# Where the unit matrix of an attention and feed-forward kernel is built: VectorE instead of GpSimd, with a new order and new buffer numbers

## The chip, the cores and the metric

The kernel runs on one core of a Trainium2 chip. A core has five engines that run beside each other, each through its own list of instructions in order: TensorE (PE in the profile, PEld for its loading of weights), VectorE (DVE), ScalarE (ACT), GpSimd (POOL) and SyncE (SP). They wait for each other through semaphores. POOL and SP, and at the end ACT, also issue DMAs. The metric is the time of one execution in microseconds (us); less is better. Several executions are given, and one more execution was recorded by the profiler.

## The reference

Attention with a decay by a forget gate, over 8 batches of 8 heads with 576 rows of 64, and behind it a gated feed-forward layer of width 1536 on the 4608 rows of 512 that come out:

```python
scores = scale * np.matmul(q, k.transpose(0, 1, 3, 2))
cum = np.cumsum(np.log(np.clip(f, 0.0001, 1.0)), axis=-1)
scores = np.where(causal, -1e9, scores + cum[:, :, :, None] - cum[:, :, None, :])
attn = np.exp(scores - np.max(scores, axis=-1, keepdims=True))
attn = attn / (np.sum(attn, axis=-1, keepdims=True) + 1e-09)
x = np.matmul(attn, v)                       # (B, H, S, D), then rows of H * D = 512
xn = x / np.sqrt(np.mean(x * x, axis=-1, keepdims=True) + 1e-06) * rms_g
g = xn @ w_gate
out = (g * (1.0 / (1.0 + np.exp(-g))) * (xn @ w_val)) @ w_out
```

## The kernel before

**A list of units.** The function builds 1956 units. A unit is a step on one engine with the units it depends on, an emitter that writes its instructions, and the buffers that it takes and gives back. Pieces of work in the code are named by what makes them: `load_qk` and `load_v` issue loads (q and k on POOL, L333 and L345 in the profile, v on SP or POOL, L356), `turn` transposes q and k by DMA from SP (L436), `turn_pe` transposes the first two batches' q and k on TensorE with the unit matrix (L451 and L457), `score_block` multiplies q and k (L526), takes the exponential on ScalarE (L545) and masks the diagonal block on POOL (L553), `scale_v` multiplies v with the decay (L486), `values` multiplies the weights with v (L574) and divides on VectorE (L593, L597), `norm` scales the rows (L619 to L636), `gate` makes the two products with w_gate and w_val (L831), and then `th` on ScalarE (L843) and two steps on VectorE, `ga` (L845) and `hT` (L838); `seven` does the same for the later groups with seven products in place of eight (L766 to L817), and `project` makes the last product (L909) with its sums on VectorE (L919) and copies on ScalarE (L916).

**The order is written out by hand.** `ORDER` gives each unit, in the order in which they are built, its rank in one list, as a number of two letters. `Plan.run` walks through the units by rank, and each engine gets its own instructions in that order. No engine can do a later unit before an earlier one of its own.

**The buffers are written out too.** A `Hold` is one use of one buffer out of a ring: `ff` are banks of PSUM for TensorE's results (4, and 8 once the scores are done and their ring `sc` is given back), `qk` 12 tiles that the loads of q and k fill, `th`, `ga`, `PT`, `xn`, `x`, `ores` and others are tiles in SBUF. `SLOTS` has one digit (or letter) for each of the 1298 Holds in the order in which the units were built: which buffer of its ring it gets. Two of the rings, `hw` and `sw`, are lanes for DMAs in the plan alone and stand for no memory. Whoever writes into a buffer waits until all who used it in its former use have ended; that is how a digit becomes a wait. Walked through by rank, the digits of before give out the free buffer of the ring that has been free longest: this holds for all rings, with 4 exceptions among the 333 banks and one on each of the two lane rings.

**A gate's banks.** A `gate` takes two Holds of `ff`, `hg` for the product with w_gate and `hv` for the one with w_val. `hg` is given back by `ga`, which comes after `th`; `hv` by `hT`, which comes after `ga`.

**The start.** f is loaded first on SP. Its decay runs through VectorE (L283), ScalarE's Ln (L285), VectorE's running sum (L291 and after) and ScalarE's Exp (L300); TensorE turns it with the fp32 unit matrix `ident_f` (L309). The transposes of q and k need the bf16 one, `ident`. Before, `make_identity` on POOL fills `ident_f` with a memset (masks.py:197) and an affine_select (masks.py:199), behind four DMA issues and ahead of the fifth; `mhalf`, a constant of -0.5, is set behind it (L271), and VectorE casts `ident_f` to `ident` (L274).

Of the kernel before, what the change touches and what calls it, by code (L numbers as in the profile page):

```python
# [32 lines left out]
WEIGH_ACT = "gv"  # L33
LETTERS = string.digits + string.ascii_letters
ORDER = (
    "0302000105060407080e090r0w0j0m0p0q0x0f0g0D1u120a0b0h0i0c0d0n0o0k0l0u0v0J0K0F0G0N0O0z0A14151v1w1G1H26"
    "272A2B2m2n35363m3n0V0W0s0t1Q1R1l1m1a1b0R0S2T2U2h2i3b3c3h3i2Y2Z3r3s3w3x3Y3Z4q4r45465q5r3N3O4x4y5R5S4L"
    "4M505164654T4U4F4G6h6i6l6m6d6e7B7C6O6P6B6C8n8o7j7k6V6W7H7I70718k8l7P7Q8V8W7p7q9U9V9C9D7N7Oa7a8b9baak"
    "alaDaEaBaC9M9N9w9xapaqbCbDadaebjbkc0c1bGbHdrdscgchdkdlcxcycEcFfsftcNcObqbrdVdWexeydadbdedfdEdFdzdAgb"
    "gceYeZeUeVgqgrg1g2fEfFgmgnf1f2e2e3g8g9hrhsgNgOjcjdiuivhDhEhShThQhRjajbiziAiniohkhljUjViXiYhxhyh0h1kv"  # L40
    "kwkgkhl4l5kLkMkQkRlElFlHlIlxlymmmn0y0C0B0E0I0H0M0Z0P0T0L0Q0Y1019131g1s1h1j1p1q1t1A111c1d1f1k1z1D1K1P"
    "1Z1V211C1N0U0X2G2s2j252a2u2f20231I1O472p2v2L2y2P302V3T3t393k3v3V4p4f4k41424a4b3M4V5f5a4B4C4O4P615x5E"
    "5I5H5N6a60695i5j55566q6k5c5d5u5v6F6g6p6v6A5C5D5K5L7F6M747b6Y7c7i7r7y67685W5X8e7D7K7R7Z8784896K6L7d7e"
    "948d8r8j7m7n75769o9b8C8K939c9h7U7V7u7v8N9j9u9p9v81829q9r9F9J9Oa29A9B9H9IaIanaFaOavaLaPaWa0a1ahaib2b4"
    "bbbgbfbnbSbsbWbxbyaRaSbvbZb5b6asataxcecmcscwaYaZcqcrbLcMcYd3cQdhdndwdKcAcBcIcJdidTdZedeietepeudOdPer"
    "eseMeCeHeXd5d6e0e1fXcff9fnfufrfAe8e9elemf8fDfPfLfQf5f6fkfldUg0gdg7fdfeezeAi0gugBgYgDgPgZgUfUfVggghhN"
    "hphIi4hzhWihieiigFgGh3h4gThLgzgAgKgLiTitiFiMixhXhYibicjAiSiWjgj8jrjujzjHj2j3iOiPl8jPjSk1k4kpkekUiGiH"
    "jNjOkGkzkPkFjXjYjCjDknlvkYlblClglnksktkCkDlOlulJlBm4kVkWl9lalVlXm3m9lhlilLlMnmmfmkmsmpmymFmImtmumgmh"
    "nzmTn4ndn1nenknhnv1618171e1n1x1o1y1L1X1S1W292e2g2o2O2R3234383g3e3l4t4z4E4Y4R534Z575Q6b6o6x6J796Z777G"
    "7T7X858a8g8h8m8q8t8v8z9n9t9G9K9L9Qa3a9aJaQb8blbmbtbpbwbzbEc8cjcPcUcXd1dgdjdxdCegejeEeLePeSf0f4fBfJge"  # L50
    "giglgHgsgygJgVhohthAhGiwiIiNiViUj0jEjMjRjWk7kdkfkokqkAkHkKlklzlAlPlQm8lZm5memimomEmwmBmHmPn3ncnJnMo6"
    "oaomot1i1r1B1F1J1E1M1T1Y22282d2l2t2x2E2I2M2S2XcKeGgji6i73B3E3I3X4Q4W3R4l4u5Y5T626G6Q6T6f6H6X98cnk6kb"
    "kc8u8f8x929e9f8G8L8M8w8D8H8O8Y8Z8Q9697a6acd7eeefaAaVaXbPbUbVb3c2c3bFbKbOccckclc6cacbfjfohakkkldLdIdR"
    "eaeNeOeTfyfzfcfafhfxfHfIfCfNfOhmiamCn9nahdh8hghUipiqhFhJhKi1j1j6jljojpjejvjwkal2ldlRlSk3kxkBkXlsltl6"
    "m6m7l0lUmzmNmRmSmMmYmZntnEpXpZq0mXnbnip4pppqo7oLoMnXoeoiosp0p1oNoToUq1qpqEqIqJ1U2k242b2r2c2w2q2z2D2C"
    "2F2H2K2N333D3q3A3J3P3a4m3f664K5t5y2J3j2Q313p3y3Q3H3S3W2W3u373d3C3o3L3z3F43583K4X494S524A44484v4j4n4J"
    "3G4h3U4c4s4o4I4w4D5e404e4d4g4i6y4H6U5p7f6R6N6u5z6c5M5U6j5g6s5B5G6D7l7L7x7E7W788y7A7M8F636w6n6r6E5b5l"
    "5m5s5w727w7a7g7J7S837Y888b8s8E8A8P918R9g959i9m7h7s7o7t7z868i8c8p8BbRcic9cdcp9P9Z9W9Ya4a5ajagamarb0bh"
    "b7bdboabazaoayaHbubJbAbIbTczcRcHcLd09TaNaaawbebBbNbMbQbXcocGcvcDddbYcuc5c7cCauaGaKaMaUf3gxfffmgEcZdm"
    "d4d8dvevfbeDf7fidteqdDdSewdNenekeBeFd9dJdudydQfSgofYgagtfvfWfGfRg3d2dBdcdodHeIfpeQeWfwgRh2h6h9hedGe5"  # L60
    "dMe4echOifidigimgIh7gMgShciJj9iQj7jjhiilhvi2iyhbhChqhwhMhHhZhPhVi5hfhuhjhnhBj4jTjkjxk8iZjmj5jqjtjyjL"
    "jGjIjQi3jsi9iCjBgCgWgQgXh5llmLmVnwk2njnQn2nAmAmGnPlTnunynDnLnGnKnTo2o4oco5ojnpnIodoknSnZo9oHoloooKow"
    "nOnYonozohoQoBoGmOnlmUn8nqk9l7kmkrljmrnNmxmQo0kEl1kIkOlcngnxnonBnHkulNkNlflWlGmalYmbmvlomjlwlDmqnFnV"
    "oCorpIpLpCpFpUq2q8q7qeqmqcqypPpYqlqoqdqaqkqwquqAqPqFqbqjqCqKqzqTqHqMnCnRoqoynWofovpgoAoFpjoPnUo3p2pd"
    "obouoEpkp5prpopBo1ogoWpHr1r5pfpuo8opoOoRoxoJp7p6pipAptpKoDoVpwpzpyoYpcpMpspJpQqioIpGpOqspTqhq4q9pVqg"
    "qNqqq3qfqrqvqBqnqtqYqQqVrdr9rcrfrjrsrorkrnryrtrzrCrFr7rJrirHsisls1s5qGqOr0r4qUr2rargrmrprlrvqDqRr6rq"
    "r3qWqZrNrerurVrBqXr8rKrMsasprArDrrrwrRrUrGrErLs9sesksgsorWs6suswsvsjsnsGsxsAsLsOrXsHsKsVsMsQsBsDrbrx"
    "sCrTrPs0rSsfstshsqsssEsJsSthsTsYsNsXt6t3t7tktdtgtstpsyt9tttytatxtltotwtAtmtqtKtEtGtztQtUtJtYtFtPtTu9"
    "u4tWu3ufukusuiuCtNuuuguPtSunujuvsRsWsZt2t1t8tftetLtRtnu2tbtitHtZtutrtvuhtOu5uluttctBuyuNuduqucue4N5A"
    "59805h5J5n5O545k5o5P8T8U5F5Z5V6t6z6I9R9S6S739k9l909acVcW8I9d8Saf8J8X9z9Xdpdq999y9s9EaTb1ijikbcbieJeK"  # L70
    "c4ctcScTdYeoe6fTdXe7ebehg4g5fgfqeRfMfKfZiDiEg6gkgvgwgfgpjhjihhisiLiRi8iriBiKjJjKjfjnjFjZk0k5lplqkiky"
    "mcmdkSkZm0m1kjlKl3lrkJkTlelmn6n7m2mlmDmJmKn0p8p9n5nnnrnsmWnfq5q6oXp3papeoSoZpbphplpmpvpxpnpDpEpNpRpS"
    "pWqxuaubqLqSsbscrhrZrQs2rIrOrYs4s7s8s3sdsmsrszsFuLuMsUt0t4t5sIsPu6u7tjtDtMuztCtItVtXu0u1u8uoumurupux"
    "uAuBuGuSuVuWuwuFuJuKuEuQuIuYuDuHuRuXv1v2uZv0uOuTuUv4v3v6v9vavhviv7vgvkvlvnvovjvrvuvvvwvxv5v8vdvevbvc"
    "vfvmvpvqvsvt")
SLOTS = (
    "751b7a63624352207908611307523743413263122050114766530534220172616310531a3810792b42666701745572212243"
    "5338606b7011595a02420533041643272850316b41377033792a11060370412562024453190b11565a707768322423423b52"
    "015566330970324741101a182264036302557113221173001561043120301100167312010541010321067011001454310732"
    "1011601200501741054321001017350016201454210702130011340016133105410107201036201610170147161105455103"  # L80
    "6012064017101456710360130101220107031014525101610234001071050230142011463106310204610751061560134137"
    "0101207107054016537011401320201071060352042231221111001352140030230101224125321243053200153343503020"
    "1235300110352232340353111431320223421335110022113311201203304200320110220163127152120231071011314170"
    "5261420107310025311042735031060220313133111010032113300020023002111001131111110030020011311003003311"
    "2200110113110110101113112100100130012010113111010331030102101021120010310210003011200121103101030132"
    "1013110201011012002110131002010301231013100231112113301030000100311130112000200131120163451704341012"
    "0110210010000012101301112113100051040720161115630227647015206514613001657356472010032116403740051617"
    "0760211043235670610104017671415011244056532102102430322217412120004531311261321023230243076222101235"
    "20120232612014360203173122105235354314317120731055051054421034363034027512103206507321410743523656")
# [66 lines left out]
def fox_ffn_kernel(ctx, tc, q, k, v, f, moe_w_gate, moe_w_val, moe_w_out, moe_rms_g, out):  # L156
    nc = tc.nc
    B, H, S, D = q.shape
    assert (B, H, S, D) == (8, 8, 576, 64)
# [114 lines left out]
    iden = dve(0.23, -19, lambda: nc.vector.tensor_copy(ident, ident_f), [iden_f])  # L274
# [10 lines left out]
    d2 = act(0.7, -19, lambda: nc.scalar.activation(fr, fr, ACT.Ln), [d1])  # L285

    def emit_cum():
        ones = bass.AP(tensor=one.tensor, offset=one.offset, ap=[one.ap[0], [0, S]])
        nc.vector.memset(one, 1.0)
# [3 lines left out]
        nc.vector.tensor_scalar_mul(mid, mid, 0.5)  # L293
# [6 lines left out]
    d4 = act(0.9, -19, lambda: nc.scalar.activation(dec[:, 0:S], cum, ACT.Exp, scale=-1.0, bias=mid[:, 0:1]),  # L300
             [d3])
# [761 lines left out]
```

## Time and profile before

| | us |
|---|---|
| median of 3 executions | 357.12 |
| lowest and highest | 354.87, 357.41 |
| the profiled execution, its own time | 354.97 |
| its span, first to last instruction | 353.1 |

The mean granted clock of TensorE in the profiled execution is 0.995 of full speed. In the profile "x4314" is a number of instructions, "PE ff L831" is TensorE writing the tile ff from line 831 of the kernel, and "<-" in a wait names what ended it. An idle time in brackets stands ahead of an instruction. A row by stage has the stretch, its length, and then the busy time of PE, PEld, DVE, ACT and POOL with the number of instructions, the granted clock, the DMA share (over 1 where the engines hold more than one packet each) and GB/s. The end of a matmul is modelled, so a busy PE need not be PE at its peak. Buffer numbers are left out in the profile; which bank a matmul writes is read from SLOTS.

### The profile page before, as it was taken

The page shows a single profiled execution, that of the slowest core. Times are in us where ns is not written, and L with a number is a line of the kernel's source. Part 1 is how long each engine was busy: PE and PEld are TensorE (multiplying, and loading weights), DVE is VectorE, ACT ScalarE, POOL GpSimd, SP SyncE. Part 2 cuts the span into 40 slices and gives each one's busy share as a digit, 9 for nine tenths or more (in the row PEclk, how much of TensorE's full clock was granted, in tenths as well). Part 3 has the DMA queues.
Part 4 walks back from the last instruction along what each step waited for, and adds up shares of the span by engine and source line. Part 5 has one row for each costly group of instructions (what it writes and reads, how often), then busy time and mean ns, then how long its engine had stood idle before and what let it go on. Part 6 is the DMA issues. An engine that isn't in the chain of part 4 may idle for free.

```text
span 353.1 us, 10559 instructions
## 1 busy us (share of the span) xinstructions
PE 334.1 (95%) x4314; PEld 259.9 (74%) x4314; DVE 275.9 (78%) x507; ACT 266.6 (75%) x440; POOL 205.8 (58%) x247
## 2 busy tenths in 40 slices
PE   1699999999999999999999999899999999999995
...
DMA  9999999899999999999999999963013200100225
GB/s 126 205 215 226 188 184 132 154 162 158 111 161 177 148 147 172 178 127 159 149 163 162 170 171 116 163 136 87 23 23 89 69 7 2 62 7 24 93 90 148
DMA packets 159464, 44.88 MB, mean 127 GB/s; under 512 B 145012, under 2 KB 158840, under 8 KB 159416
## 3 DMA queue, kind: packets, MB, share of 16 engines
...
q8 instruction: 33, 0.54, 0.7%
...
## 4 chain that ended last, share of the span: by engine, by line
PE 79%; POOL 6%; DVE 5%; DMA 4%; issue 2%; ACT 1%; SPq 1%; DVEq 0%; POOLq 0%
PE ff L831 29%; PE ff L909 16%; PE late L766 9%; PE ff L766 8%; PE ff L574 6%; PE sc L526 6%; PE late L909 5%; DMA qk<-in_k_dram 2%; DMA xT<-xn 1%; POOL qk L333 1%; ACT PT L545 1%; DMA v<-in_v_dram 1%; POOL PT L553 1%; DVE hT L838 1%; POOL Vs L486 1%
## 5 line engine op out<-in xcount | busy, mean ns | idle before, releaser
L545 ACT ACTIVATE PT<-sc 128x1024 bf16<-128x1024 f32 x96 | 94.9, 1021 | 15.8 <-PE sc L526 15.6
L831 PE MATMUL ff<-xT,wv 128*128 128x128 bf16 (+2 forms) x464 | 68.6, 291 | 0.6 <-DVE hT L838 0.4
L831 PE MATMUL ff<-xT,wg 128*128 128x128 bf16 (+2 forms) x464 | 68.0, 291 | 0.7 <-DVE ga L845 0.5
L817 POOL TENSOR_TENSOR hT<-PT,PT 128x512 bf16<-128x512 f32 x20 | 25.9, 1301 | 53.6 <-ACT PT L811 33.0
L845 DVE SCALAR_TENSOR_TENSOR ga<-th,ff 128x512 f32<-128x512 f32 x68 | 46.1, 682 | 12.3 <-ACT th L843 11.2
L838 DVE SCALAR_TENSOR_TENSOR hT<-ga,ff 128x512 bf16<-128x512 f32 x68 | 46.0, 684 | 11.2 <-PE ff L831 10.0
L553 POOL TENSOR_SCALAR_AFFINE_SELECT PT<-PT 128x1024 bf16<-128x1024 bf16 x32 | 37.3, 1166 | 27.1 <-ACT PT L545 26.9
L843 ACT ACTIVATE th<-ff 128x512 f32<-128x512 f32 x68 | 39.8, 595 | 13.5 <-PE ff L831 8.8
L831 PEld LDWEIGHTS <-wg 128*128 128x128 bf16 x464 | 36.4, 98 | 18.5 <-issue 0.8
L831 PEld LDWEIGHTS <-wv 128*128 128x128 bf16 x464 | 36.1, 98 | 18.3 <-issue 0.9
L909 PEld LDWEIGHTS <-hT 128*128 128x128 bf16 x432 | 41.4, 98 | 5.9
L486 POOL TENSOR_TENSOR Vs<-v,decT 128x512 bf16<-128x512 f32 (+1 forms) x30 | 33.1, 1105 | 18.8 <-DMA v<-in_v_dram 18.7
L574 PEld LDWEIGHTS <-PT 128*128 128x128 bf16 (+1 forms) x896 | 32.0, 102 | 9.5 <-issue 2.8
L574 PE MATMUL ff<-Vs,PT 128*128 128x65 bf16 (+1 forms) x896 | 36.8, 196 | 1.3 <-POOL Vs L486 0.9
L597 DVE TENSOR_TENSOR x<-ff,rden 128x256 f32<-128x256 f32 (+1 forms) x80 | 33.9, 424 | 2.7
L909 PEld LDWEIGHTS <-sm 128*128 128x128 bf16 x324 | 31.2, 98 | 6.1 <-issue 1.3
L526 PE MATMUL sc<-QT,KT 64*128 64x128 bf16 (+1 forms) x960 | 32.8, 212 | 0.7 <-ACT PT L545 0.6
L526 PEld LDWEIGHTS <-KT 64*128 64x128 bf16 x960 | 24.0, 96 | 10.9 <-issue 9.0
L333 POOL DMA_DIRECT2D qk<-in_q_dram x34 | 29.9, 882 | 0.8 <-POOLq L1047 0.8
L333 POOL DMA_DIRECT2D qk<-in_k_dram x34 | 29.9, 880 | 0.1
L909 PE MATMUL ff<-wo,hT 128*128 128x256 bf16 x240 | 29.3, 273 | 0.0
L919 DVE TENSOR_TENSOR ores<-ores,ff 128x512 f32<-128x512 f32 (+1 forms) x35 | 23.4, 669 | 7.6 <-PE ff L909 7.2
...
## 6 DMA issues: line engine op xcount, KB each, us to landing
...
wo<-in_moe_w_out_dram POOLq DMA_DIRECT2D x2, 768.0 KB, 10.5
```

What stands on the lines that cost most here:

```text
L333: nc.gpsimd.dma_start(out=T_qk[h.slot][0:n, :].rearrange("p (h d) -> p h d", d=D), in_=src[b, :, p0:p0 + n, :].rearrange("h p d -> p h d"))
L486: eng.tensor_tensor(T_Vs[hv.slot][0:n, j, :, 0:D], T_v32[h.slot][0:n, :, :], bcast(dj, D), ALU.mult)
L526: nc.tensor.matmul(t[:, par, c:c + n], lhsT=kt[r, p, kj * 128:(kj + 1) * 128], rhs=qt[r, p, qi * 128:qi * 128 + n], start=not x, stop=True ...
L545: nc.scalar.activation(T_of_p[hp.slot][:, 0:2 * half].rearrange("p (a c) -> p a c", a=2)[:, :, 0:cols], T_sc[h.slot][:, :, 0:cols], ACT.Ex ...
L553: nc.gpsimd.affine_select(out=d, in_=d, pattern=[[0, 8], [1, n]], compare_op=ALU.is_ge, fill=0.0, base=0, channel_multiplier=-1)
L574: nc.tensor.matmul(T_ff[hpo.slot][r0:r0 + n, p * 65:p * 65 + 65], lhsT=T_of_p[h.slot][:, c:c + n], rhs=vs[:, kj, 2 * p + par, :], start=(k ...
L766: nc.tensor.matmul(t[:, c * HTK:(c + 1) * HTK], lhsT=w[:, d, (2 * u + c) * 128:(2 * u + c + 1) * 128], rhs=r[:, d, :], start=(start and c ...
L831: nc.tensor.matmul(T_ff[h.slot][:, c:c + n], lhsT=w[:, dc, fc * 128:(fc + 1) * 128], rhs=xT[:, dc, t0:t0 + n], start=(dc == 0), stop=(dc = ...
L838: nc.vector.scalar_tensor_tensor(hT, in0=three[0], scalar=0.5, in1=three[1], op0=ALU.mult, op1=ALU.mult)
L843: th = act(0.6, key - 0.1, lambda: nc.scalar.activation(T_th[ht.slot], T_ff[hg.slot], ACT.Tanh, scale=0.5), [ug], take=[ht])
L845: a = dve(0.69, key - 0.1, lambda: nc.vector.scalar_tensor_tensor(T_ga[ha.slot], in0=T_th[ht.slot], scalar=1.0, in1=T_ff[hg.slot], op0=ALU ...
L909: nc.tensor.matmul(t[:, s * HD:(s + 1) * HD], lhsT=a()[:, fc, s * 128:(s + 1) * 128], rhs=w[:, fc, :], start=(not more and s == ss[0] and ...
```

## The change

The unit matrix is built on VectorE. A running count along the columns (a scan over ones) gives 1 to 32 in each row, a transpose of blocks of 32x32 gives the same count down the rows, and where the two are equal the bf16 matrix gets a 1; four such comparisons fill the four blocks on the diagonal of a zeroed tile. `ident_f` is cast from `ident`, where before it was the other way. `mhalf` is set on VectorE too, and the memset of `one` moves there from `emit_cum`, which now depends on this unit. POOL has no part of it any more.

```diff
-from concourse.masks import make_identity
...
-    one = sb.tile([BH, 1], F32, name="one")
+    one = sb.tile([128, 1], F32, name="one")
+    diag = sb.tile([128, 64], F32, name="diag")
...
     def emit_ident():
-        make_identity(nc, ident_f)
-        nc.gpsimd.memset(mhalf, -0.5)
-
-    iden_f = pool(0.7, -15.5, emit_ident)
-    iden = dve(0.23, -19, lambda: nc.vector.tensor_copy(ident, ident_f), [iden_f])
+        along, down = diag[:, 0:32], diag[:, 32:64]
+        nc.vector.memset(one, 1.0)
+        ones = bass.AP(tensor=one.tensor, offset=one.offset, ap=[one.ap[0], [0, 32]])
+        nc.vector.tensor_tensor_scan(along, ones, ones, 0.0, ALU.mult, ALU.add)
+        nc.vector.transpose(down, along)
+        nc.vector.memset(ident, 0.0)
+        for c in range(0, 128, 32):
+            nc.vector.tensor_tensor(ident[c:c + 32, c:c + 32], along[c:c + 32, :], down[c:c + 32, :], ALU.is_equal)
+        nc.vector.memset(mhalf, -0.5)
+
+    iden = dve(1.2, -25, emit_ident)
+    iden_f = dve(0.2, -19, lambda: nc.vector.tensor_copy(ident_f, ident), [iden])
...
     def emit_cum():
-        ones = bass.AP(tensor=one.tensor, offset=one.offset, ap=[one.ap[0], [0, S]])
-        nc.vector.memset(one, 1.0)
+        ones = bass.AP(tensor=one.tensor, offset=one.offset, ap=[[one.ap[0][0], BH], [0, S]])
...
-    d3 = dve(2.5, -19, emit_cum, [d2])
+    d3 = dve(2.5, -19, emit_cum, [d2, iden])
```

The strings ORDER and SLOTS are replaced as a whole. Read unit by unit, the new ORDER keeps TensorE's 485 units and SP's in the same order, POOL's too apart from the unit matrix that is gone, and on VectorE and ScalarE moves one unit each past a neighbour; the unit matrix now stands near the top of VectorE's list, behind one memset of a KT tile. The new SLOTS gives, walked through by rank, each Hold the free buffer of its ring with the highest number (332 of 333 banks, and all of the other rings). The ninth line of SLOTS, which the prediction speaks of, before and after:

```diff
-    "2200110113110110101113112100100130012010113111010331030102101021120010310210003011200121103101030132"
+    "3001311030110211311023112011201021101310122112001121013003311211032111210131133112110221000310131022"
```

More of the change, by code (lines that the diff above doesn't have):

```diff
@@ L35 @@
 ORDER = (
[L36 to L75, printed above, removed]
-SLOTS = (
[L77 to L84, printed above, removed]
-    "2200110113110110101113112100100130012010113111010331030102101021120010310210003011200121103101030132"
[L86 to L89, printed above, removed]
@@ new lines @@
+    "00010203040d0507080c09060h0i0m0o0p0v0e0k0B1t110a0l0f0q0b0g0n0t0j0r0u0E0H0Q0D0N0L0U0x0K131h1v1H1F1R26"
+    "2i2B2K2l2z333j3k3y0T150s0A1P221k1w191m0P0Z2T362g2v3a3o3g3t2X3d3p3C3u3F3Y4c4q4G444h5p5x3N404w4M5Q5X4I"
+    "524X5c626b4Q574C4V6e6o6j6x6c6r7C7K6M716C6P8m8r7i7s6U777I7Q6Z7e8l8v7N7V8T997m7z9Sa19A9N7M80a6afb8biai"
+    "axaAaJazaP9J9Y9v9CaoaEbAbQacakblbxbZcbbFbMdodCcfcsdidrcxcLcDcRfrfBcJcZbpbDdWe1eweNd9dpdddmdDdQdydKg9"
+    "gheWf9eTf3gpgvg4gjfGfRgkgrf0fee0ebg6gchrhEgJh0j5jeisiIhBhPhRi0hOi5jdjqiwiEiliChkhyjUk1j2jghwhLgYh5ks"
@@ new lines @@
+    "kGkfkvl3lbkMkVkQl2lylHlKm0lBlOmhmo0w0z0y0C0G0F0J0X0M0R0I0O0W0Y18121e1r1f1i1n1q1s1z101a1b1d1j1y1C1J1O"
+    "1Y1U1Z1B1M0S0V2F2q2h25292s2e20231G1N432n2t2L2x2P2Y2U3S3q383h3s3U4p4d4k3X4b474i3M4S5d584z4P4K50635w5C"
+    "5H5G5M685Z675h5s535e6p6g5a5l5t5E6F6f6m6v6A5B5L5J5S7D6L72796W7a7g7o7v666k5U658e7B7H7O7X8682886J6V7c7n"
+    "938d8p8j7k7x747h9m9b8C8K909a9f7S837r7G8M9i9t9n9u7Z899p9y9D9G9La09z9I9F9RaGalaCaNaraKaOaV9Zabagatb1b3"
+    "babebdbmbSbqbVbvbJaRb0bubYb4bfapaBaucdcjcpcvaXb7cocAbIcIcVd2cNdedkdvdIcycKcFcSdfdSdXeaeheqenerdOdYes"
@@ new lines @@
+    "eBeJezeFeVd5dhdZe9fVcef6flftfqfye5egeleuf7fDfMfIfNf2fgfjfwdTfZgag2fbfoeyeLhYgugzgWgCgMgXgSfTg5gdgohK"
+    "hohGi3hvhTigicihgEgQh2hcgRhJgwgGgLgZiUiqiBiLiuhVi7ibimjxiQiTjjj8jpjtjyjFiYj9iNiWlajNjRjXk3knkdkSiFiR"
+    "jMjYkEkxkOkCjZk7jEjLkklwkWl8lIlflmkqkDkAkLlPlslClxm6kTl6l7lilWlRm4m9lglqlElNnnmgmmmtmqmAmFmImlmvmbmk"
+    "nymSn3nbmZndnjngnu1416171c1l1u1o1x1K1W1Q1V282d2f2m2O2R3032353e3b3i4s4x4B4U4N4Z4W545P6a6l6w6I766X737E"
+    "7R7U848a8g8h8k8o8s8u8z9l9s9E9H9K9Oa2a7aHaQb6bjbkbrbobtbwbBc7cgcMcQcUd0dcdgdwdAeeeieCeHeKeReXf1fzfFgb"
@@ new lines @@
+    "gfglgFgqgxgIgThnhqhxhDitiDiMiXiSiZjBjJjQjTk6kckeklkokykFkJljlAlvlQlMm7lVm3mfmimpmEmwmBmHmPn2nanHnMo7"
+    "o9onot1g1p1A1E1I1D1L1S1X21272c2k2r2w2D2H2M2S2WcGeEggi4if3z3D3I3W4L4R3Q4l4t5W5R606E6N6R6d6G6T95ckk5kb"
+    "km8t8f8x8Y9d9o8G8L8V8w8D8H8N8W988P949ga5aad6edeoayaUaWbNbUc3b2c0c9bCbHbOcacicuc4c8clfifmh9kikwdJdGdP"
+    "e6eMeYeSfxfJfaf5fffvfEfQfAfLfXhli9mCn8nkhdh7hghQinizhChHhUhWj0j7jljojzjfjujGkal0lclLlXk2ktkzkUlrlDl4"
+    "lYmakYlUmymNmRn0mMmXn7nsnIpWpZq9mWn9nhp2popvo6oKoTnXoeoiosoYpboMoSp3q0qqqEqIqP1T2j242a2p2b2u2o2y2C2A"
@@ new lines @@
+    "2E2G2J2N313B3n3x3J3O374m3c644H5r5v2I3f2Q2Z3m3v3P3H3R3V2V3r34393A3l3L3w3E41553K4T464O4Y4y42454u4j4n4F"
+    "3G4f3T484r4o4E4v4A5b3Z4a494e4g6y4D6S5o7b6O6K6t5y695K5V6h5f6q5A5F6B7j7J7u7A7T758y7y7L8E616u6i6n6D595j"
+    "5k5q5u6Y7t787d7F7P817W878b8q8F8A8O8Z8Q9e929h9k7f7p7l7q7w858i8c8n8BbRchc6cccn9M9X9T9Wa3a4ahaeajanaYbg"
+    "b5bbbna9awamavaFbsbGbybEbTcwcOcEcHcX9QaMa8asbcbzbLbKbPbWcmcCctcBdbbXcrc2c5czaqaDaIaLaTeZgyfcfkgDcWdj"
+    "d4d7dtetf8eAf4fhdqepdBdRevdMekejexeDd8dHdsdxdNfPgmfWg7gtfsfUfCfOg1d1dzdadldFeGfneOeUfugPh1h4h8hedEe2"
@@ new lines @@
+    "dLe4echMidiaieikgHh6gKgOhbiGj6iOj4jchiijhthZivhahAhphuhIhFhXhNhSi2hfhshjhmhzj1jSjijvk8iVjkj3jnjsjwjI"
+    "jDjHjOi1jri8iyjAgBgUgNgVh3lkmLmUnvk0ninRn1nAmzmGnPlTntnxnDnLnEnKnTo2o4oco5ojnpnGodoknSnZoaoHoloooLow"
+    "nOnYomozohoPoBoGmOnlmTn6nqk9l5kjkplhmsnNmxmQo1kBkZkHkNl9nfnwnonCnJkrlGkKlelZlzmcm1mdmulnmjltlFmrnFnV"
+    "oCoqpIpLpCpFpTq1q6q5qeqmqbqypPpYqlqoqcq8qkqwquqAqRqFqaqjqCqJqzqTqHqLnBnQoroynWofovpgoAoFpjoOnUo3p0pc"
+    "obouoEpkp4pppnpBo0ogoUpHr1r5pfpto8opoNoQoxoJp6p5pipApspKoDoVpwpzpyoXpapMprpJpQqioIpGpOqtpSqhq3q7pUqg"
```

23 lines of the change are left out of this document (added).

## The prediction

> **What bounds the kernel now.** I read the page first, then the busy times by stage, the waits, the start of the chain of waits, and last the timeline.
>
> ```profile
> span 353.1 us, 10559 instructions
> ...
> PE 334.1 (95%) x4314; PEld 259.9 (74%) x4314; DVE 275.9 (78%) x507; ACT 266.6 (75%) x440; POOL 205.8 (58%) x247
> ...
> PE   1699999999999999999999999899999999999995
> ...
> DMA  9999999899999999999999999963013200100225
> ```
>
> ```profile
> 8.00:17.00 9.00, 6.12 (x96) 4.85 (x94) 4.74 (x12) 6.00 (x6) 9.00 (x11) 0.97 1.67 204
> ...
> 31.00:100.00 69.00, 68.29 (x1178) 61.49 (x1176) 60.45 (x113) 63.96 (x106) 46.27 (x60) 1.00 1.40 159
> 100.00:200.00 100.00, 100.00 (x1209) 61.86 (x1204) 75.58 (x145) 78.25 (x127) 72.75 (x91) 1.00 1.52 160
> 200.00:300.00 100.00, 96.67 (x1124) 76.49 (x1122) 82.25 (x144) 76.03 (x135) 44.05 (x48) 1.00 0.54 84
> 300.00:353.00 53.00, 48.97 (x447) 43.32 (x444) 35.40 (x55) 24.69 (x46) 14.18 (x11) 1.00 0.22 71
> ```
>
> TensorE is the bound from about 31 us to the end: in the rows by stage (stretch, length, then busy PE, PEld, DVE, ACT, POOL, the clock, the DMA share) it is idle 0.7 us of 69, 0 of 100, 3.3 of 100 and 4.0 of 53. Its order is fixed by hand, so whatever makes it wait there comes out at the end.
>
> ```profile
> PE ff L451 <- DVE ident L274: 7.1, 1, 7.1
> ...
> PE ff L909 <- DVE hT L838: 0.9, 1, 0.9
> ```
>
> Its waits (total, times, longest) say the same: one of 7.1 us for the unit matrix at the start, and every other one is short. The start is the place that the change is about:
>
> ```profile
> 5.06 0.22 POOL ident_f masks.py:197
> ...
> 5.35 1.30 POOL ident_f masks.py:199
> ...
> 11.04 5.66 DMA qk<-in_k_dram
> ```
>
> In the chain of waits (start, us) the unit matrix holds POOL from 5.06 to 6.65 us, between two DMA issues, and a later load of k is what TensorE waits for next.
>
> **The change part by part: the unit matrix.** POOL loses a memset, an affine_select and the memset of mhalf: 1.6 us, and no DMA of POOL or SP changes its place, so every load from the third k load on can be issued 1.6 us earlier. If all of it reached the end it would bring 1.65 us. I count little of it, because the DMA engines are full: 9 tenths in nearly all of the first 26 slices, and 1.67 packets per engine in the row for 8 to 17 us. A load issued earlier then stands in the DMA queue instead of on POOL.
>
> ```profile
> 3.62 0.84 DVE L283 TENSOR_SCALAR hT<-hT 64x576 f32<-64x576 f32 x1 [1.09 <-DMA hT<-in_f_dram]
> 4.41 0.06 DVE L289 MEMSET one<- 64x1 f32 x1
> ...
> 6.85 0.21 DVE L274 CAST ident<-ident_f 128x128 bf16<-128x128 f32 x1
> 6.96 0.77 ACT L300 ACTIVATE hT<-hT,mid 64x576 f32<-64x576 f32 x1 [0.26 <-DVE mid L293]
> 7.11 1.12 PE L451 MATMUL ff<-ident,qk 128*128 128x128 bf16 x8 [7.11 <-DVE ident L274]
> ...
> 7.61 0.35 PEld L451 LDWEIGHTS <-qk 128*128 128x128 bf16 x4 [0.18 <-DMA qk<-in_k_dram]
> ...
> 8.15 0.80 PE L309 MATMUL ff<-ident_f,hT 64*128 64x64 f32 x5
> ```
>
> The first transposes no longer wait for ident at 7.11, but those of k still wait for the load of k (7.61), issued before the unit matrix; so the first scores, which need k, stay where they are. VectorE gets ten small instructions ahead of L283 (three memsets, a scan and a transpose over 32 columns, four comparisons of 32x32, the cast, of which the cast only moves). No row shows the transpose or the comparison; between the 0.06 of L289 and the 0.21 of L274 each, ten cost 0.6 to 2.1 us. VectorE stands idle 1.09 us before L283, so L283 comes 0 to 1.0 us later, and the decay behind it has 0.42 us to spare (L300 ends at 7.73, L309 reads it at 8.15): 0 to 0.6 us lost. I take 0.11 each, which the idle time covers. The unit matrix together: from -1.65 to +0.6, and I take -0.5, nearer to nothing because of the full DMA engines.
>
> **The digits of SLOTS.** The diff also replaces ORDER and SLOTS. ORDER leaves TensorE's order, SP's, and POOL's apart from the unit matrix as they were. SLOTS does not stay: before, the digits give out the buffer that has been free longest; after, always the free one with the highest number, often the one just let go. For the PSUM ring ff (4 banks until the scores end) this counts, because the matmul waits until VectorE or ScalarE has emptied its bank. An example, with its rows:
>
> ```profile
> 105.13 0.60 ACT L843 ACTIVATE th<-ff 128x512 f32<-128x512 f32 x1 [0.29 <-PE ff L831]
> 105.15 0.81 PE L831 MATMUL ff<-xT,wg 128*128 128x512 bf16 x3
> ...
> 105.76 0.69 DVE L845 SCALAR_TENSOR_TENSOR ga<-th,ff 128x512 f32<-128x512 f32 x1 [0.85 <-ACT th L843]
> 105.80 1.03 PE L831 MATMUL ff<-xT,wv 128*128 128x512 bf16 x4
> ...
> 106.86 0.69 DVE L838 SCALAR_TENSOR_TENSOR hT<-ga,ff 128x512 bf16<-128x512 f32 x1 [0.41 <-PE ff L831]
> ...
> 106.90 1.67 PE L831 MATMUL ff<-xT,wg 128*128 128x512 bf16 x7
> ```
>
> Digits 42, 43 and 46 of the ninth line of SLOTS are the banks of this gate's wg product, its wv product and the next gate's wg product: 1, 3, 1 before, 2, 2, 2 after. So the wv product, which started at 105.80, has to wait for L845 to read the wg product out of the same bank until 106.45: 0.65 us. L838, which had waited 0.41 us for that wv product, moves with it, and the next wg product, begun at 106.90, waits for L838's end (107.55): 0.65 us again. Those two add.
>
> I set this beside the trace for all 305 PSUM banks that TensorE takes a second time: start of its first matmul less the end of the last read of the bank's former content, each from the profiled run. With the old digits none is short: the smallest is 0.052 us, the median 0.84. With the new ones 118 are short, by 38.9 us in sum, 0.33 on average. The first big one and the last, with their rows:
>
> ```profile
> 15.28 0.41 PE L574 MATMUL ff<-Vs,PT 128*128 128x65 bf16 x8
> 15.82 0.42 DVE L597 TENSOR_TENSOR x<-ff,rden 128x256 f32<-128x256 f32 x1
> 321.99 1.28 DVE L807 TENSOR_TENSOR hT<-th,late 128x512 bf16<-128x512 f32 x2
> 322.80 0.82 PE L909 MATMUL ff<-wo,hT 128*128 128x256 bf16 x6
> ```
>
> The second four of the eight at 15.28 (they start at 15.41) go into the bank that L597 reads until 16.24: 0.84 short. L909 at 322.80 takes the bank that L807 reads until 323.27: 0.48.
>
> They do not all add. While VectorE works off a backlog its ends stay where they are when TensorE slips, and one wait pays for the next; where it had stood idle for TensorE's result, it slips too.
>
> ```profile
> DVE ga L845 <- ACT th L843: 11.2, 15, 1.7
> DVE hT L838 <- PE ff L831: 10.0, 22, 1.0
> ```
>
> So I cut the trace at each idle gap over 0.1 us of the reading engine and keep only the largest shortfall of a stretch: 67 stretches, by stage 1.6 (to 31 us), 5.2 (to 100), 10.3 (to 200), 5.5 (to 300), 2.1: 24.7 us. Each wait also ends 0.052 us after the release, the smallest distance above: 3.5. Bank waits 28.2. The lower bound lets every read start as soon as its data are there, as if its engine had no backlog: 10.6 us are short even then. The upper one adds all: 38.9 + 118 x 0.052 = 45.
>
> [...]
>
> **SLOTS on POOL.** The qk ring is hit too: 25 loads on POOL get a tile whose transposes had not landed, 67.6 us short in sum, where before none had under 11 us to spare.
>
> ```profile
> KT<-qk SPq DMA_TRANSPOSE x32, 4.3
> ```
>
> ```profile
> 151.21 4.71 SPq L436 DMA_TRANSPOSE KT<-qk  x3
> 152.17 0.89 POOL L333 DMA_DIRECT2D qk<-in_q_dram  x1
> ...
> 159.10 0.19 POOL L627 TENSOR_SCALAR ms<-sq 128x2 f32<-128x2 f32 x1 [0.71 <-ACT junk L622]
> ...
> 160.96 0.66 POOL L553 TENSOR_SCALAR_AFFINE_SELECT P<-P 128x512 bf16<-128x512 bf16 x1
> ...
> 162.06 0.20 PEld L574 LDWEIGHTS <-PT 128*64 128x64 bf16 x8 [0.42 <-issue]
> ```
>
> The load at 152.17 needs the transpose issued at 151.21; at the median of 4.3 it lands at 155.5, so POOL stands 3.3 us, and L486, L627 and the mask L553 stand behind it. POOL's idle 0.71 gives some back, the mask has 0.44 to spare (161.62 to 162.06): 2.2 us reach TensorE. Three places are like this (near 112, 152, 182 us): 0 to 6.5, and I take 3, as TensorE is late there anyway. The rings xn, th, PT and ores get tighter too, on ScalarE and VectorE; without a row for it I take 1, between 0 and the same 3.3.
>
> Sum, against the profiled run's own 354.97 us (span 353.1, 2.2 under the median 357.12): 354.97 - 0.5 + 28.2 + 3 + 1 = 386.7, so 387.
>
> **The rivals.** (1) ScalarE and VectorE catch up while TensorE waits, and only the lower bound stays: 354.97 - 0.5 + 10.6 = 365. For it: to 100 us nearly all shortfalls are backlog (10.5 short, 0.6 without it). Against it: from 100 to 200 us VectorE is busy only 75.6 of 100 and stands idle again and again. (2) Not slower: the new digits' waits fall into time in which TensorE is idle anyhow, and the loads come 1.65 us earlier: 353.3. The place would be the 19 us that TensorE isn't busy; but 7.1 of them are the start, and after 31 us it is 8 in all. It decides only if the waits stay under these 8 plus the 1.65, and the stretch from 100 to 200, where 47 takes are short, has no idle time. (3) POOL becomes the bound: from 100 to 200 us it is busy 72.75, and 43.5 us of the short loads lie there, 116 in 100: 16 us over, 387 + 16 = 403. Against it: a late POOL finds its tiles landed. (4) Nothing overlaps: 118 x 0.684 (the 0.69 of L845 above) = 81, 436. Against it: the average shortfall is half that.
>
> **How the numbers follow.** Forecast (374 to 400) 0.63; rival 1 (358.5 to 374) 0.20; rival 2 0.09; rival 3 0.06; rival 4 0.02. The range: at the bottom 354.97 - 1.65 + 10.6 = 364, at the top 354.97 + 0.6 + 45 + 6.5 + 3.3 = 410, of which I take 409; it leaves out rivals 2 and 4 and the lower part of rival 1, about 0.18. About 1% is what a measurement of this kernel can tell from no change; faster by more is 0.02, within it 0.07 (both rival 2), slower 0.91.
>
> **What would show it.** Right: waits of TensorE for L845, L838, L593 or L597 on ff, 20 us or more in sum; its busy time in 100 to 200 us below 95; POOL issues L333 that wait for the DMA of QT or KT; the unit matrix on VectorE before 3.6 us, the first transposes near 5.7, but k's at 7.6 as before. Wrong: TensorE fully busy from 31 us on as now (rival 2), or waits of TensorE for L553 and L486 that outweigh those for banks (rival 3).

## The result, and the profile after

| | us |
|---|---|
| before, median of 6 executions beside the changed kernel | 357.26 |
| after, median of 6 executions (400.99 to 403.62) | 403.04 |
| ratio | 1.127, 95% interval 1.123 to 1.132 |
| the profiled execution of after, its own time | 403.62 |
| its span | 401.6 |

The change costs 45.8 us. The prediction said slower, 387 us in a range of 364 to 409. The direction and the range held. The time lies past the stretch of 374 to 400 that the prediction gave most chance to, and the rise was about half as large again as the sum's 30. Lines behind the unit matrix have numbers higher by 7 now: L831 is L838, L838 is L845, L843 is L850, L845 is L852, L597 is L604, and the load of q and k is L340.

The page of after, its busy times, slices and clock:

```profile
span 401.6 us, 10540 instructions
...
PE 349.1 (87%) x4287; PEld 266.2 (66%) x4314; DVE 279.5 (70%) x515; ACT 268.1 (67%) x440; POOL 204.2 (51%) x244
...
PE   3689979997988968899988978978998999998984
...
PEclk9999999999999996999999999999999999999999
```

TensorE, 95% busy before, is 87% busy in a longer span, and the slices that are not 9 are spread over all of it: no single stall, but many. The rows by stage (columns as before):

```profile
31.00:100.00 69.00, 62.96 (x1098) 56.45 (x1095) 54.80 (x105) 58.67 (x93) 42.00 (x53) 0.99 1.36 142
100.00:200.00 100.00, 88.50 (x1027) 57.37 (x1039) 63.80 (x121) 65.40 (x108) 61.37 (x78) 0.96 1.14 130
200.00:300.00 100.00, 88.83 (x1080) 59.75 (x1093) 76.40 (x139) 73.45 (x124) 52.70 (x62) 1.00 0.78 113
```

From 100 to 200 us TensorE is busy 88.5 where it was busy 100. Taking the same weight load of TensorE in both traces, after is behind by 4.1 us at 31 us of before's time, by 14.2 at 100, 31.9 at 200, 42.3 at 300. Of the 4.1 us, 1.9 are found in the profiled run with the old digits too (first experiment below), so these are not the digits'. VectorE and ScalarE do the same work in more time (busy 63.8 and 65.4 of these 100 us, where it was 75.6 and 78.3). What is new or has grown are waits (total, times, longest):

```profile
POOL qk L340 <- DMA KT<-qk: 33.3, 13, 7.7
...
POOL qk L340 <- DMA QT<-qk: 17.3, 8, 4.3
...
PE ff L838 <- DVE ga L852: 6.3, 12, 1.8
...
PE ff L838 <- DVE x L604: 5.7, 9, 3.2
...
PE ff L838 <- DVE hT L845: 5.2, 9, 1.1
...
PE sc L533 <- ACT PT L552: 3.6, 4, 1.6
...
PE ff L581 <- POOL Vs L493: 2.0, 2, 1.8
```

TensorE waits for a bank that VectorE has not emptied yet; with the further, shorter rows that name L852, L845 or L604 it is 22.6 us in all, where the same rows of before make 2.4. POOL stands 50.6 us at loads of q and k, waiting for transposes by DMA, where before it did not wait for one. The waits are not all of the loss: TensorE's busy time rose too, by 15.0 us. A matmul of 512 columns takes 0.38 us alone (the last row below), while in a row they follow each other every 0.22 us (seven take 1.67 at 106.90 in the prediction's example: six times 0.215, and 0.38). The last one ahead of a pause counts as busy for the whole 0.38, so a pause costs an estimated 0.16 us more than its idle time. TensorE's list of waits has 72 in place of 12: 60 times 0.16 is an estimated 10 of the 15 us, and the phases of half clock (see What the hardware showed) hold up to 4.4 more. The gate that the prediction took as its example, in the timeline of after:

```profile
118.47 1.92 PE L838 MATMUL ff<-xT,wg 128*128 128x512 bf16 x7
...
120.28 0.69 DVE L852 SCALAR_TENSOR_TENSOR ga<-th,ff 128x512 f32<-128x512 f32 x1 [0.96 <-ACT th L850]
...
121.02 1.02 PE L838 MATMUL ff<-xT,wv 128*128 128x512 bf16 x4 [0.62 <-DVE ga L852]
...
122.08 0.69 DVE L845 SCALAR_TENSOR_TENSOR hT<-ga,ff 128x512 bf16<-128x512 f32 x1 [1.11 <-PE ff L838]
...
122.82 0.38 PE L838 MATMUL ff<-xT,wg 128*128 128x512 bf16 x1 [0.54 <-DVE hT L845]
```

The wv product starts 0.05 us after L852 has read the wg product out of the same bank (120.97), and the next wg product 0.05 us after L845 (122.77). These are two waits that add, as foretold at 0.65 each. They have 0.62 and 0.54 of idle time, and each an estimated 0.16 more for the matmul that ran out ahead of it. And the start of after:

```profile
1.10 0.22 DVE L274 TENSOR_TENSOR_SCAN diag<-one 128x32 f32<-128x32 f32 x1
...
1.36 0.21 DVE L275 STREAM_TRANSPOSE diag<-diag 128x32 f32<-128x32 f32 x1
...
1.68 0.77 DVE L278 TENSOR_TENSOR ident<-diag 32x32 bf16<-32x32 f32 x4
...
2.52 0.06 DVE L279 MEMSET mhalf<- 128x5 f32 x1
...
5.65 0.61 PE L458 MATMUL ff<-ident,qk 128*128 128x128 bf16 x4 [5.65 <-DMA qk<-in_q_dram]
...
6.54 0.61 PE L458 MATMUL ff<-ident,qk 128*128 128x128 bf16 x4 [0.29 <-DMA qk<-in_k_dram]
...
8.00 0.79 PE L316 MATMUL ff<-ident_f,hT 64*128 64x64 f32 x5 [0.85 <-ACT hT L307]
...
8.92 0.61 PE L533 MATMUL sc<-QT,KT 64*128 64x128 bf16 x8
```

The unit matrix is there at 2.5 us and nothing waits for it any more. But the first scores come at 8.92 instead of 9.08: the decay (L316, waiting 0.85 us for ScalarE's L307) is what holds TensorE next.

### The profile page after: what moved, and what is told of

Read it like the earlier page. It is cut to its first block, busy times and chain, and to the rows that moved or that the text cites. A ratio compares the mean times of both kernels' runs of the same rounds, so it can differ in the third digit from the quotient of the medians.

```text
span 401.6 us, 10540 instructions
## 1 busy us (share of the span) xinstructions
PE 349.1 (87%) x4287; PEld 266.2 (66%) x4314; DVE 279.5 (70%) x515; ACT 268.1 (67%) x440; POOL 204.2 (51%) x244
## 5 line engine op out<-in xcount | busy, mean ns | idle before, releaser
L838 PE MATMUL ff<-xT,wv 128*128 128x128 bf16 (+2 forms) x454 | 70.4, 295 | 10.6 <-DVE x L604 4.3
L838 PE MATMUL ff<-xT,wg 128*128 128x128 bf16 (+2 forms) x447 | 68.3, 290 | 8.7 <-DVE hT L845 3.5
L852 DVE SCALAR_TENSOR_TENSOR ga<-th,ff 128x512 f32<-128x512 f32 x68 | 46.2, 682 | 21.5 <-ACT th L850 20.1
L845 DVE SCALAR_TENSOR_TENSOR hT<-ga,ff 128x512 bf16<-128x512 f32 x68 | 46.0, 684 | 20.8 <-PE ff L838 19.6
L850 ACT ACTIVATE th<-ff 128x512 f32<-128x512 f32 x68 | 39.9, 595 | 28.4 <-PE ff L838 21.8
L838 PEld LDWEIGHTS <-wv 128*128 128x128 bf16 x464 | 37.6, 99 | 30.2 <-issue 13.7
L838 PEld LDWEIGHTS <-wg 128*128 128x128 bf16 x464 | 37.1, 98 | 28.3 <-issue 12.2
L560 POOL TENSOR_SCALAR_AFFINE_SELECT PT<-PT 128x1024 bf16<-128x1024 bf16 x32 | 35.5, 1110 | 34.0 <-ACT PT L552 33.9
L340 POOL DMA_DIRECT2D qk<-in_k_dram x34 | 29.7, 876 | 33.0 <-DMA KT<-qk 19.2
L581 PEld LDWEIGHTS <-PT 128*128 128x128 bf16 (+1 forms) x896 | 34.0, 104 | 15.1 <-issue 7.6
L581 PE MATMUL ff<-Vs,PT 128*128 128x65 bf16 (+1 forms) x896 | 38.1, 198 | 5.6 <-POOL Vs L493 2.0
L340 POOL DMA_DIRECT2D qk<-in_q_dram x34 | 29.8, 879 | 18.6 <-DMA KT<-qk 14.1
L916 PEld LDWEIGHTS <-sm 128*128 128x128 bf16 x324 | 31.2, 98 | 10.5 <-issue 4.5
L533 PE MATMUL sc<-QT,KT 64*128 64x128 bf16 (+1 forms) x960 | 33.7, 215 | 3.8 <-ACT PT L552 3.6
L604 DVE TENSOR_TENSOR x<-ff,rden 128x256 f32<-128x256 f32 (+1 forms) x80 | 33.9, 424 | 3.4 <-ACT xn L643 0.4
L493 POOL TENSOR_TENSOR Vs<-v,decT 128x512 bf16<-128x512 f32 (+1 forms) x30 | 33.6, 1120 | 4.6 <-DMA v<-in_v_dram 4.4
L643 ACT ACTIVATE xn<-x,rs 128x512 bf16<-128x512 f32 (+1 forms) x38 | 27.0, 719 | 13.2 <-POOL rs L635 9.0
L533 PEld LDWEIGHTS <-KT 64*128 64x128 bf16 x960 | 24.9, 97 | 13.8 <-issue 11.9
L600 DVE RECIPROCAL rden<-ff 128x4 f32<-128x4 f32 x72 | 12.8, 177 | 20.8 <-PE ff L581 20.3
```

Source lines behind the costliest of these rows:

```text
L340: nc.gpsimd.dma_start(out=T_qk[h.slot][0:n, :].rearrange("p (h d) -> p h d", d=D), in_=src[b, :, p0:p0 + n, :].rearrange("h p d -> p h d"))
L493: eng.tensor_tensor(T_Vs[hv.slot][0:n, j, :, 0:D], T_v32[h.slot][0:n, :, :], bcast(dj, D), ALU.mult)
L533: nc.tensor.matmul(t[:, par, c:c + n], lhsT=kt[r, p, kj * 128:(kj + 1) * 128], rhs=qt[r, p, qi * 128:qi * 128 + n], start=not x, stop=True ...
L560: nc.gpsimd.affine_select(out=d, in_=d, pattern=[[0, 8], [1, n]], compare_op=ALU.is_ge, fill=0.0, base=0, channel_multiplier=-1)
L581: nc.tensor.matmul(T_ff[hpo.slot][r0:r0 + n, p * 65:p * 65 + 65], lhsT=T_of_p[h.slot][:, c:c + n], rhs=vs[:, kj, 2 * p + par, :], start=(k ...
L604: nc.vector.tensor_tensor(d, po[r0:r0 + n, :, 0:D], bcast(r[r0:r0 + n, :], D), ALU.mult)
```

## The experiments

All ran on the chip beside the kernel before (medians 356.4 to 357.5). "Costs" is the difference of the two medians. The digits of SLOTS fall into three groups: the banks ff (256 digits changed), the load tiles qk (62), and all other rings (631). An experiment gives the new digits to some rings and leaves the old ones to the others; the diffs are against the line named.

**The two halves of the change.** First the new unit matrix with all of SLOTS as before; then the old unit matrix with the new ORDER and SLOTS (its own two units kept at their old places). The ninth line of SLOTS of the first, against after:

```diff
-    "3001311030110211311023112011201021101310122112001121013003311211032111210131133112110221000310131022"
+    "2200110113110110101113112100100130012010113111010331030102101021120010310210003011200121103101030132"
```

> The changed kernel (unit matrix on VectorE, new ORDER) with the SLOTS of before. My theory: the digits are the whole loss, and the unit matrix is worth 0.5 us: 356 to 357, that is within 1% of the kernel before (357.26), TensorE busy all through from 100 to 200 us, no wait for L852, L845 or L604 over 1 us in sum; the first transposes near 5.7, the first scores within 0.3 us of the 9.08 of before. Rival, the 1.6 us of POOL reach the end: 355.6 or less. Rival, the unit matrix or the new ORDER carries part of the loss: over 361.

Measured: 357.27, ratio 0.999 (0.996 to 1.002).

The second has the new digits, and POOL's unit matrix of before; against after:

```diff
-        nc.vector.memset(one, 1.0)
...
-        nc.vector.memset(mhalf, -0.5)
+        make_identity(nc, ident_f)
+        nc.gpsimd.memset(mhalf, -0.5)
```

> The kernel before, unit matrix on POOL, with the new SLOTS and the new ORDER (the two units of the unit matrix kept at their old places in it). My theory: the loss is all there, 401 to 405, as the changed kernel (403.04). Rival, the unit matrix on VectorE carries part of it: under 398.

Measured: 402.86, ratio 1.129 (1.124 to 1.134), as after. The unit matrix, for which the change is named, is worth nothing that can be measured; the digits are the whole loss. With the old digits TensorE is full again:

```profile
100.00:200.00 100.00, 100.00 (x1227) 62.22 (x1225) 75.99 (x145) 76.86 (x126) 72.30 (x89) 1.00 1.51 160
```

**The unit matrix on POOL, three times.** Against before:

```diff
-        make_identity(nc, ident_f)
+        for _ in range(3):
+            make_identity(nc, ident_f)
```

> The kernel before, but with the unit matrix on POOL made three times over, 3.2 us more between the fourth and the fifth DMA issue. My reason for counting 0.5 us of 1.65 was that the DMA queue is full there. If so, the fifth load's issue can slip by about 1.0 us before it shows (it took 5.34 us to land where the first load took 4.33) and the first transposes are late by 3.2: together 2.2 us more, 359 to 360. Rival, all of POOL's time counts: 360.5 or more. Rival, nothing of it counts: 357 to 358.

Measured: 357.65, ratio 1.000 (0.997 to 1.004). In its timeline the repeats were cheap:

```profile
5.35 1.30 POOL masks.py:199 TENSOR_SCALAR_AFFINE_SELECT ident_f<-ident_f 128x128 f32<-128x128 f32 x1
...
6.98 0.29 POOL masks.py:199 TENSOR_SCALAR_AFFINE_SELECT ident_f<-ident_f 128x128 f32<-128x128 f32 x1
```

So POOL's fifth issue came at 7.90 in place of 6.64, the first transposes at 8.21, 1.1 us later than before, and the first scores at 10.07, 1.0 later. That is less than the 3.2 us that were meant, and even this does not show in the time: the 359 to 360 of the theory did not come, and the rival of 357 to 358 did.

**The banks alone.** New digits for ff, the old ones for the rest; the ninth line against the old digits:

```diff
-    "2200110113110110101113112100100130012010113111010331030102101021120010310210003011200121103101030132"
+    "3000310130110210311123112000200121011310122112010121013103301211132011210130033012100221100301130122"
```

> The changed kernel with the new digits for the PSUM ring ff alone (256 digits), the old ones for all other rings. My sum: 28.2 us for the banks, so 385 (between 367 and 401). Rival, the banks are worth the upper bound and all shortfalls add: 400 or more, which leaves nothing for the other rings. Rival, ScalarE and VectorE catch up and the other rings carry most of the 45.8 us: under 370.

Measured: 385.08, ratio 1.078 (1.074 to 1.082): 27.6 us, where the prediction had 28.2. Its waits and its row by stage:

```profile
PE ff L838 <- DVE ga L852: 4.3, 10, 0.7
...
PE ff L838 <- DVE hT L845: 3.7, 8, 1.0
...
PE ff L581 <- DVE x L604: 3.4, 4, 2.3
...
PE ff L838 <- DVE x L604: 2.5, 8, 0.7
```

```profile
100.00:200.00 100.00, 92.94 (x1075) 57.96 (x1073) 68.52 (x132) 71.43 (x116) 66.84 (x84) 1.00 1.27 147
```

By stage the lag behind the old digits grew by 0.5 us (to 31 us), 3.7 (to 100), 10.4 (to 200), 9.4 (to 300) and 2.7, against 1.6, 5.2, 10.3, 5.5 and 2.1 of the prediction's stretches (its 3.5 us for releases are not spread over them). So the sum is closer than its parts: less came to 100 us than foretold, more from 200 to 300, where the granted clock dropped in the slice from 248.8 to 258.4 us (8 tenths in the clock row of its page), a loss of 1.9 at most.

**The load tiles alone.** New digits for qk; the first line of SLOTS, in which most of them stand:

```diff
-    "751b7a63624352207908611307523743413263122050114766530534220172616310531a3810792b42666701745572212243"
+    "751b7a63624352207b0a611307523743413263122050114b6a530938220b7661671a531433107925426a6b01785972292743"
```

> The changed kernel with the new digits for the ring qk alone (62 digits). My sum: 3 us (0 to 6.5), so 360 (357 to 364); POOL waits at the issues of q and k for transposes for some tens of us in sum, and little of it reaches TensorE. Rival, POOL carries the part that my sum lacks (15.9 us of the measured loss): 370 to 376.

Measured: 375.14, ratio 1.050 (1.045 to 1.054): 17.7 us, the rival's number and six times what the prediction gave. Its waits:

```profile
POOL qk L340 <- DMA KT<-qk: 42.8, 15, 7.3
...
ACT xn L643 <- POOL rs L635: 17.3, 6, 6.1
POOL qk L340 <- DMA QT<-qk: 16.8, 6, 4.7
...
PE ff L581 <- POOL Vs L493: 4.7, 2, 2.5
...
PE ff L581 <- POOL PT L560: 3.6, 3, 1.4
...
PE ff L916 <- DVE ga L852: 3.5, 1, 3.5
...
PE ff L581 <- POOL P L560: 2.5, 1, 2.5
...
PE sc L533 <- DMA QT<-qk: 0.7, 1, 0.7
```

POOL stands 59.6 us. What it has behind the wait comes late: the norms, whose rs ScalarE awaits for 17.3 us in all, and the scaled v and the masks, for which TensorE waits 4.7 and 6.1. Scores that wait for a transpose hardly show (0.7). One place where a norm reaches TensorE, in the timeline:

```profile
219.45 0.94 POOL L340 DMA_DIRECT2D qk<-in_q_dram  x1 [4.25 <-DMA KT<-qk]
...
220.73 0.71 POOL L635 TENSOR_TENSOR rs<-ms,mhalf 128x2 f32<-128x2 f32 x1
221.48 0.72 ACT L643 ACTIVATE xn<-x,rs 128x512 bf16<-128x512 f32 x1 [6.09 <-POOL rs L635]
...
222.71 0.69 DVE L852 SCALAR_TENSOR_TENSOR ga<-th,ff 128x512 f32<-128x512 f32 x1 [4.00 <-ACT th L850]
...
223.45 2.07 PE L916 MATMUL ff<-wo,hT 128*128 128x256 bf16 x12 [3.48 <-DVE ga L852]
```

POOL waits 4.25 us, issues the load, and only then gets to rs, for which ScalarE has stood 6.09 us. The th that ScalarE has behind this xn comes late, with it VectorE's ga, and TensorE stands 3.48 us for the bank that ga gives back.

**All other rings.** New digits for every ring but ff and qk; the ninth line against the old digits:

```diff
-    "2200110113110110101113112100100130012010113111010331030102101021120010310210003011200121103101030132"
+    "2201111013110111101013112111101030102010113111001331030002111021020110310211103111210121003110031032"
```

> The changed kernel with the new digits for all rings but ff and qk (631 digits: th, PT, xn, x, ores, v32 and the rest, and the lanes that stand for no memory). My sum: 1 us (0 to 3.3), so 358, 357 to 361. Rival, they carry part of the loss: over 363.

Measured: 367.56, ratio 1.032 (1.026 to 1.037): 10.5 us, where the prediction had 1. The new waits are on ScalarE, for tiles that others still read:

```profile
ACT PT L552 <- PE ff L581: 7.1, 7, 2.7
...
ACT th L850 <- DVE ga L852: 5.6, 7, 1.5
...
ACT xn L643 <- DMA xT<-xn: 4.5, 2, 2.5
```

None of the three stands among the waits of the kernel with the old digits. Two of the rings, PT and th, were then tried by themselves (172 digits; the same line):

```diff
-    "2200110113110110101113112100100130012010113111010331030102101021120010310210003011200121103101030132"
+    "2200111113110110101113112110101130112010113111000331030002111021120110310211003111210121103111031132"
```

> The new kernel with the new digits for the rings PT and th alone (172 digits: what ScalarE writes for TensorE and VectorE), the old ones for all others. All rings but ff and qk cost 10.3 us together. Theory: ScalarE, waiting for a PT that TensorE still reads or a th that VectorE still reads, brings most of it: 363 to 367. Rival: the scores' ring sc, the norms' xn and the output's ores bring most, and PT and th alone stay at 357 to 362.

Measured: 361.00, ratio 1.011 (1.006 to 1.015): 4.0 of the 10.5 us. My theory fell; the larger part comes from the rest (sc, xn, ores, x and more) or from PT and th together with it. That was not taken apart further.

**Two groups at a time.** The same lines with the digits of ff and qk; of ff and the others; of qk and the others:

```diff
+    "3000310130110210311123112000200121011310122112010121013103301211132011210130033012100221100301130122"
...
+    "3001311030110211311023112011201021101310122112001121013003311211032111210131133112110221000310131022"
...
+    "2201111013110111101013112111101030102010113111001331030002111021020110310211103111210121003110031032"
```

> The changed kernel with the new digits for ff and for qk, the old ones for all other rings. My theory by now: the two losses add (27.6 for the banks alone, 17.7 for qk alone, over the 357.3 of the old digits) and no other ring counts: 402.6, between 400 and 405. Rival, the waits overlap (a TensorE that waits for banks gives POOL the time that it lost): under 396, and the rest of the changed kernel's 403.0 then comes from the other rings.

> The new kernel with the new digits for every ring but qk, which keeps the old ones. Theory: the three groups share their waits, so that a group that joins the others adds less than it costs alone (17.7 us for qk). The banks and the other rings together then lie between the larger of the two alone and their sum: 357.3 + 27.6 = 385 to 357.3 + 27.6 + 10.3 = 395, and qk adds the rest to the 403 of the changed kernel, 8 to 18 us. Rival: the banks' waits hide those of the other rings wholly or the two multiply, so that the time falls outside 385 to 395.

> The new kernel with the new digits for every ring but the banks ff, which keep the old ones. Theory: qk and the other rings strike different engines (POOL, and ScalarE with VectorE) and nearly add: 357.3 + 17.7 + 10.3 = 385, and the banks add 18 us to that in the changed kernel, less than their 27.6 alone. Rival: they overlap as the banks and qk did (33.0 in place of 45.3), which gives 357.3 + 0.73 x 28.0 = 378, and then the banks bring their nearly full 25 us in the whole.

| new digits for | us | ratio, interval | costs | sum of its parts alone |
|---|---|---|---|---|
| ff and qk | 390.44 | 1.092 (1.085 to 1.099) | 33.3 | 45.3 |
| ff and others | 392.35 | 1.099 (1.094 to 1.104) | 35.9 | 38.1 |
| qk and others | 385.63 | 1.082 (1.077 to 1.087) | 29.2 | 28.2 |
| all three (after) | 403.04 | 1.127 (1.123 to 1.132) | 45.8 | 55.8 |

The waits of banks and of load tiles share 12 us, so the first theory, that they add, fell and its rival held; that what one of them makes late gives the other time is the likely reason, not shown by itself. The other rings come nearly in full on top of either, and the other two theories held. In the whole, then, taking a group away saves 16.6 (ff), 9.9 (qk) or 12.5 us (others), each to within 2 or 3 us.

**How the load tiles cost so much.** Two attempts to tell the standing POOL (A) from the late loads (B). In the first, the 25 loads that wait stand later in ORDER; the first line that differs:

```diff
-    "2i2B2K2l2z333j3k3y0T150s0A1P221k1w191m0P0Z2T362g2v3a3o3g3t2X3d3p3C3u3F3Y4c4q4G444h5p5x3N404w4M5Q5X4I"
+    "2i2B2K2l2z333j3k3y0T150s0A1P221k1w191m0P0Z2T362g2v3a3o3g3t2X3d3p3C3u3F3Y4c4v4w444h5n5v3N404O4P5Q5X4H"
```

> As the run with the new digits for qk alone (375.1), but in ORDER each of the 25 loads of q and k whose tile was not free yet is moved behind the POOL work that stood behind it, to the place where its tile has come free by the trace of the run with the old digits; two of them stop earlier, ahead of the transpose that needs them. Theory A: the 17.7 us come from what stands behind the waiting load on POOL (masks L560, Vs L493, rs L635): 357 to 362. Theory B: they come from the loads themselves being late, and the transposes and scores after them: 371 or more, as the loads are no earlier here.

Measured: 378.61, ratio 1.065 (1.057 to 1.074). The number is that of the late loads, but the run tells nothing apart. All 25 stand later in the list, but an engine sees only its own part of it, and in POOL's only 11 of them came behind work that is no load. So POOL still stood 52.9 us at L340, and TensorE still waited 10.1 us for the masks and the scaled v of POOL. In the second, the digits are the old ones, and POOL waits behind each of the 25 loads for the transposes that the load would have waited for:

```diff
+                if (b, nm, j) in BEHIND:
+                    nc.gpsimd.memset(T_qk[hold_qk[BEHIND[b, nm, j]].slot][0:1, 0:1], 0.0)
```

> The new kernel with the old digits for all rings. Behind each of the 25 loads of q and k that the new digits make wait, POOL writes one element of the tile whose transpose that load would have waited for; the tile's content has been used by then, so nothing that is computed changes. POOL then stands still about as long as with the new digits (60 us in sum), but the load on which it would have stood is already issued. Theory A, what POOL has behind the wait (masks, scaled v, norms) costs the time: 370 to 376, as with the new digits for qk alone (375.1). Theory B, the late loads themselves cost it, since their transposes and then the scores come late: 357 to 362.

Measured: 364.13, ratio 1.023 (1.017 to 1.029): 7.7 us, between the two. Its waits (POOL's element is written by L370; L581 and L560 are L610 and L589 there):

```profile
POOL qk L370 <- DMA QT<-qk: 15.1, 6, 3.4
POOL qk L370 <- DMA KT<-qk: 14.7, 6, 6.5
...
PE ff L610 <- POOL P L589: 2.5, 1, 2.5
```

The same transposes were waited for at the same places of POOL's list, but POOL stood 29.8 us and not 59.6. So with the loads on time POOL stands half as long, and that costs 7.7 us. The other half arose only where the load itself was held up; that the later transposes, on which later loads wait, came late with it is the likely reason, not shown by itself. The traces say how the 10 us that it brings reach TensorE. Its waits for POOL's masks and scaled v are 0.4 us with the old digits, 3.5 here and 10.8 with the late loads, where the 3.48 us behind the late norm come on top. From 31 to 300 us the granted clock is 1.00 in every stage with the old digits, 0.98 in one of three here and 0.98 in all three with the late loads: none, one and three phases of half clock, which at 3.4 us each (see What the hardware showed) hold an estimated 0, 1.7 and 5.1 at most. These differences cover the 10 us, and the scores that wait for a transpose (0.7) hardly count: the path is POOL's work, as in theory A, and what makes it so long is the late load. No run takes the parts one by one.

## Why the prediction was right, and where it was off

- **What decides: the digits, and through banks.** Right for the digits, and for the banks in part: of the sum's rise they were nearly all, of the measured 45.8 us they are 16.6 to 27.6. Foretold were 20 us or more of waits of TensorE for L845, L838, L593 and L597, TensorE under 95 from 100 to 200 us, and loads of POOL that wait for the DMA of QT or KT: 22.6 us, 88.5, and 50.6 us.
- **The unit matrix, -0.5 us (-1.65 to 0.6).** Right in that it is small: with the old digits the new one is 0.2 us faster, with the new digits 0.2 slower, and both are within the noise, so that neither -0.5 nor its sign can be told. It was done by 2.6 us, and the first transposes came at 5.65. Wrong in detail: k's transposes came at 6.54 (7.12 with the old digits) and not 7.6. What keeps the gain small at the scores is the decay, which TensorE reads at 8.00, rather than k.
- **Bank waits, 28.2 us.** Right: 27.6 alone, though by stage the parts are off both ways, and that they cancel is luck. Reading the start of each bank's first matmul less the end of the last read, and keeping one shortfall for each stretch of the reading engine, carried it; the lower bound of 10.6 and the plain sum of 45 were both far off.
- **The load tiles on POOL, 3 us (0 to 6.5).** The term that was mis-sized: 17.7 alone, 9.9 in the whole. The standing itself was foretold well: 67.6 us short, 59.6 stood. The step that failed is what of it reaches TensorE. "Three places are like this" counted only masks with little to spare, and gave no price to the scaled v (4.7 us of TensorE's waits) and the norms, which ScalarE awaits (3.5 at TensorE in one place); the masks alone came to 6.1.
- **The other rings, 1 us (0 to 3.3).** Mis-sized too: 10.5 alone, 12.5 in the whole. "Without a row for it" was not so: their shortfalls could have been counted from the digits as those of the banks were. The bound of 3.3 was borrowed from another term and had no ground of its own.
- **The sum.** The terms were added without a term for sharing. Sized right they would have made 55.8, 10 too much; the two errors partly met, and the rise came out at 30 for 45.8. That the range held is partly luck: the load tiles and the other rings each went past their bounds of 6.5 and 3.3, and the room that took them in was the upper bound of 45 for the banks, which no run came near. The sum has no term for the clock either.
- **The rivals.** ScalarE and VectorE did not catch up (365), and no cover was found for the waits (353.3). POOL as the bound has the number of the result, 403, but not its mechanism: TensorE's waits for POOL are 2.0 us on the row of L493 against 22.6 for banks, and POOL is busy 61.4 of 100. Without any overlap it would have been 436: that is 81 us for the 118 short takes, where the banks alone cost 27.6.
